# Few long-lived PSUM pools with tile-wise reuse in place of many short pools, in a linear-attention and MQA forward and backward kernel

## Chip, cores, metric

The kernel runs on one core of one Trainium2 chip. The metric is the device time of one execution in microseconds (us), slowest core, so here the only one. A profile is one more execution, read by its trace; its span can differ from the median by some us.

## The reference

Two independent blocks on 2048 tokens of width 448 in bfloat16, 16 heads of 28, their outputs side by side, and all eight gradients for a given gradient of the output:

```python
def _A_ref(x, wqkv, wo):                     # linear attention
    q, k, v = split_heads(x @ wqkv)
    pq, pk = phi(q), phi(k)                  # phi(t) = where(t > 0, t + 1, exp(t)) + 1e-6
    kv = einsum("bhsd,bhse->bhde", pk, v);  z = pk.sum(over tokens)
    o = einsum("bhqd,bhde->bhqe", pq, kv) / (einsum("bhqd,bhd->bhq", pq, z)[..., None] + 1e-6)
    return merge_heads(o) @ wo
def _B_ref(x, wq, wk, wv, wo):               # one key/value head for 16 query heads
    q = split_heads(x @ wq); k = x @ wk; v = x @ wv
    p = softmax(einsum("bhqd,bkd->bhqk", q, k) * Dh ** -0.5)
    return merge_heads(einsum("bhqk,bkd->bhqd", p, v)) @ wo
def reference(...):
    out, vjp = jax.vjp(lambda *t: concatenate([A(...), B(...)], -1), *inputs)
    return (out, *vjp(grad_out))
# ... shortened: helper names stand for the reshapes and transposes
```

## The kernel before

It is one program, phase A then phase B. TensorE (PE) multiplies and transposes into PSUM, VectorE (DVE) and ScalarE (ACT) move PSUM on to SBUF, GpSimd (POOL) clears buffers, SyncE (SP) issues most DMAs. A copy that empties a PSUM tile is called an eviction. Every small stage opens its own PSUM pool, with one set of slots for each tile name, and closes it at its end. Tiles named below: in A, ps_nd (numerator and denominator), ps_oa (out_a); in B, ps_qn (norms of the queries), otp (transposes of the attention's output), ps_ob (out_b), gwoBacc (gradient of wo), ps_do (gradient of the attention's output); in both, projT, projK, projV (projections), xTps (transposes of the last 64 columns of x or of the output's gradient), tps_set (other transposes). The stage between the forward loop and the key/value loop of B, cut:

```python
with tc.tile_pool(name="psOt", bufs=2, space=PSUM) as psOt, ...:
    for g in range(4):
        for st in range(NS):
            otp = psOt.tile([P, P], F32, name="otp")
            tpz(otp[:, :], osb_all[:, g * NS + st, :], identF)         # PE transpose
            # ... DVE: copy, denominators, reciprocal, product -> onat_B
...
    with tc.tile_pool(name="psB4", bufs=3, space=PSUM) as psB4:
        transpose_set(... oT_B ..., ... onat_B ..., psB4)
        for st in range(NS):
            ps = psB4.tile([P, D], F32, name="ps_ob")
            for g in range(4):
                mm(ps[:, :], oT_B[g][:, st * P:(st + 1) * P], woB_pr[g][:, :], start=(g == 0), stop=(g == 3))
            ot = bwk.tile([P, D], BF16, name="out_b_sb")               # two buffers
            nc.any.tensor_copy(out=ot[:], in_=ps[:, :])
            nc.sync.dma_start(out0[st * P:(st + 1) * P, D:2 * D], ot[:])
...
    with tc.tile_pool(name="psBgb", bufs=2, space=PSUM) as pst:
        transpose_64col(pst, lambda st: gb_nat[:, st, 384:448], gbT[3])        # xTps
    with tc.tile_pool(name="psBB1", bufs=1, space=PSUM) as ps7:
        accs = [ps7.tile([P, D], F32, name=f"gwoBacc{g}") for g in range(4)]
        # 64 matmuls onat_B^T gb_nat; then four copies gwo_sb and their stores
    with tc.tile_pool(name="psBB1b", bufs=2, space=PSUM) as ps1:
        # per 128 tokens: ps_do = gb wo^T on PE, six DVE operations -> don2_B
        transpose_set(... doT2_B ..., ... don2_B ..., ps1)
```

Phase A and the start and end of B are built in the same way: some thirty pools. The loops in between (forward: st_ps, oacc; key/value: s_ps, dp_ps, dvT_acc, dkT_acc; query: dpt_ps, dqacc) keep one set of pools each.

Of the kernel before, what the change touches and what calls it, by code (L numbers as in the profile page):

```python
# [12 lines left out]
BF16 = mybir.dt.bfloat16  # L13
# [8 lines left out]
SKIP_A = False  # L22


@with_exitstack
def kernel(
# [90 lines left out]
    def load_xT(pool, x2d, xn, nm):  # L117
        xT = [pool.tile([P, S], BF16, name=f"{nm}_T{c}") for c in range(4)]
        for c in range(3):
            nc.sync.dma_start_transpose(xT[c][:, :], x2d[:, c * P:(c + 1) * P])  # L120
        with tc.tile_pool(name=f"{nm}_pst", bufs=2, space=bass.MemoryType.PSUM) as pst:
            transpose_64col(pst, lambda st: xn[:, st, 384:448], xT[3])
        return xT
# [30 lines left out]
    def build_woT_pad(pool, wo_pr, nm):  # L154
        tiles = []
        with tc.tile_pool(name=f"{nm}_ps", bufs=2, space=bass.MemoryType.PSUM) as pst:
            for ci in range(4):
                lo, hi = ci * P, ci * P + DC_ROWS[ci]
                t = pool.tile([P, 512], BF16, name=f"{nm}{ci}")
                ps = pst.tile([P, 512], BF16, name="woTps")  # L160
                for g in range(4):
                    tpz(ps[0:hi - lo, g * P:(g + 1) * P], wo_pr[g][:, lo:hi], identB)
                nc.vector.tensor_copy(out=t[0:hi - lo, :], in_=ps[0:hi - lo, :])
                tiles.append(t)
        return tiles
# [47 lines left out]
    def phase_A():  # L213
        pa = ExitStack()
        ain = pa.enter_context(tc.tile_pool(name="ain", bufs=1, side="left"))
# [3 lines left out]
        woT_pad_A = build_woT_pad(ain, woA_pr, "woTA")  # L219
# [23 lines left out]
        with ExitStack() as fs:  # L243
            tmp = fs.enter_context(tc.tile_pool(name="a_tmp1", bufs=1, side="right"))
            xaT = load_xT(tmp, Ax2, xa_nat, "xa")
            wqA_pad = load_w_pad(tmp, A_wqkv, 0, "wqA_pad")
            wkA_pad = load_w_pad(tmp, A_wqkv, D, "wkA_pad", nc.gpsimd)
            wvA_pad = load_w_pad(tmp, A_wqkv, 2 * D, "wvA_pad")
            with tc.tile_pool(name="psA0", bufs=4, space=bass.MemoryType.PSUM) as ps0:
                wTq = build_wT_padrows(ain, wqA_pad, "wTqA", ps0)  # L250
                wTk = build_wT_padrows(ain, wkA_pad, "wTkA", ps0)
                wTv = build_wT_padrows(ain, wvA_pad, "wTvA", ps0)
            with tc.tile_pool(name="psA1", bufs=2, space=bass.MemoryType.PSUM) as psA1:
                def evq(g, qc, ps):
                    phi_from_psum(ps[:, :], pqT_A[g][:, qc * 512:(qc + 1) * 512], (P, 512), awk)
                proj_T(psA1, lambda dc, g, rows: wqA_pad[0:rows, dc, g * P:(g + 1) * P], xaT, evq)
                for st in range(NS):
                    ps = proj_nat(psA1, xaT, st, lambda dc, rows: wkA_pad[0:rows, dc, :], 512, nm="projK_ps")
                    phi_from_psum(ps[:, :], pkn_A[:, st, :], (P, 512), awk)
                    ps2 = proj_nat(psA1, xaT, st, lambda dc, rows: wvA_pad[0:rows, dc, :], 512, nm="projV_ps")  # L260
                    nc.scalar.activation(out=vaug_A[:, st, :], in_=ps2[:, :], func=ACT.Identity)
                nc.gpsimd.memset(vaug_A[:, :, :].rearrange("p t (h c) -> p t h c", c=32)[:, :, :, 0:1], 1.0)
# [3 lines left out]
        with tc.tile_pool(name="psA2", bufs=1, space=bass.MemoryType.PSUM) as psA2:  # L266
# [14 lines left out]
        with tc.tile_pool(name="psA3", bufs=4, space=bass.MemoryType.PSUM) as psA3:  # L281
# [14 lines left out]
        with ExitStack() as fs2:  # L296
            t2 = fs2.enter_context(tc.tile_pool(name="a_oT", bufs=1, side="right"))
            oT_A = [t2.tile([P, S], BF16, name=f"oT_A{g}") for g in range(4)]
            with tc.tile_pool(name="psA4", bufs=3, space=bass.MemoryType.PSUM) as psA4:
                transpose_set(lambda g, qc: oT_A[g][:, qc * 512:(qc + 1) * 512],  # L300
                              lambda g, st: onat_A[:, st, g * P:(g + 1) * P], psA4)
                for st in range(NS):
                    ps = psA4.tile([P, D], F32, name="ps_oa")
                    for g in range(4):
                        mm(ps[:, :], oT_A[g][:, st * P:(st + 1) * P], woA_pr[g][:, :], start=(g == 0), stop=(g == 3))
                    ot = awk.tile([P, D], BF16, name="out_a_sb")
                    nc.any.tensor_copy(out=ot[:], in_=ps[:, :])
                    nc.sync.dma_start(out0[st * P:(st + 1) * P, 0:D], ot[:])
# [3 lines left out]
        with ExitStack() as bs:  # L312
# [6 lines left out]
            with tc.tile_pool(name="psAga", bufs=2, space=bass.MemoryType.PSUM) as pst:  # L319
                transpose_64col(pst, lambda st: ga_nat[:, st, 384:448], gaT[3])  # L320
            with tc.tile_pool(name="psAB1", bufs=3, space=bass.MemoryType.PSUM) as ps1:
# [19 lines left out]
                with tc.tile_pool(name="psAB7", bufs=1, space=bass.MemoryType.PSUM) as ps7:  # L341
# [11 lines left out]
            with tc.tile_pool(name="psAB1t", bufs=4, space=bass.MemoryType.PSUM) as pst:  # L353
# [5 lines left out]
        with ExitStack() as bs:  # L359
            tp_ = bs.enter_context(tc.tile_pool(name="a_pqn", bufs=1, side="right"))  # L360
            pqn_A = tp_.tile([P, NS, 512], BF16, name="pqn_A")
            with tc.tile_pool(name="psAB2t", bufs=4, space=bass.MemoryType.PSUM) as pst:
                transpose_set(lambda g, qc: pqn_A[:, qc * 4:(qc + 1) * 4, g * P:(g + 1) * P],
                              lambda g, st: pqT_A[g][:, st * P:(st + 1) * P], pst)
            with tc.tile_pool(name="psAB2", bufs=1, space=bass.MemoryType.PSUM) as ps2:
# [13 lines left out]
            with tc.tile_pool(name="psAB2b", bufs=2, space=bass.MemoryType.PSUM) as psb:  # L379
# [12 lines left out]
        with tc.tile_pool(name="psAB3", bufs=4, space=bass.MemoryType.PSUM) as ps3:  # L392
# [11 lines left out]
        with ExitStack() as bs:  # L404
            pk1 = bs.enter_context(tc.tile_pool(name="a_gkn", bufs=1, side="right"))
            gkn_A = pk1.tile([P, NS, 512], BF16, name="gkn_A")
            with ExitStack() as bs2:
                pv = bs2.enter_context(tc.tile_pool(name="a_vaugT", bufs=1, side="right"))
                vaugT_A = [pv.tile([P, S], BF16, name=f"vaugT_A{g}") for g in range(4)]
                with tc.tile_pool(name="psAB4t", bufs=4, space=bass.MemoryType.PSUM) as pst:  # L410
                    transpose_set(lambda g, qc: vaugT_A[g][:, qc * 512:(qc + 1) * 512],
                                  lambda g, st: vaug_A[:, st, g * P:(g + 1) * P], pst)
                with tc.tile_pool(name="psAB4", bufs=2, space=bass.MemoryType.PSUM) as ps4:
# [7 lines left out]
            with tc.tile_pool(name="psAB4b", bufs=3, space=bass.MemoryType.PSUM) as ps4:  # L421
# [3 lines left out]
        with ExitStack() as bs:  # L425
            pk2 = bs.enter_context(tc.tile_pool(name="a_pkT", bufs=1, side="right"))
            pkT_A = [pk2.tile([P, S], BF16, name=f"pkT_A{g}") for g in range(4)]
            with tc.tile_pool(name="psAB4c", bufs=4, space=bass.MemoryType.PSUM) as ps4:
# [8 lines left out]
        for gT, blk in [(gqT_A, 0), (gvT_A, 2)]:  # L437
            with ExitStack() as bs:
                tp_ = bs.enter_context(tc.tile_pool(name=f"a_ab5_{blk}", bufs=1, side="right"))
                gnat = tp_.tile([P, NS, 512], BF16, name=f"gnat_{blk}")  # L440
                with tc.tile_pool(name=f"psAB5_{blk}", bufs=3, space=bass.MemoryType.PSUM) as ps5:
# [4 lines left out]
        with tc.tile_pool(name="psAB6", bufs=2, space=bass.MemoryType.PSUM) as ps6:  # L446
# [28 lines left out]
    def phase_B():  # L475
        pb = ExitStack()
        bin_ = pb.enter_context(tc.tile_pool(name="bin", bufs=1, side="left"))
# [3 lines left out]
        woT_pad_B = build_woT_pad(bin_, woB_pr, "woTB")  # L481
# [13 lines left out]
        with ExitStack() as fs:  # L495
# [3 lines left out]
            xbT = load_xT(tmp, Bx2, xb_nat, "xb")  # L499
# [9 lines left out]
            with tc.tile_pool(name="psB0", bufs=2, space=bass.MemoryType.PSUM) as ps0:  # L509
# [11 lines left out]
            with tc.tile_pool(name="psB1", bufs=2, space=bass.MemoryType.PSUM) as psB1:  # L521
# [25 lines left out]
            with tc.tile_pool(name="psB2", bufs=2, space=bass.MemoryType.PSUM) as psB2:  # L547
# [17 lines left out]
                for g in range(4):  # L565
                    for qc in range(NQC):
# [5 lines left out]
                        for j in range(4):  # L572
                            nc.scalar.activation(out=qT_B[g][32 * j:32 * j + 1, qc * 512:(qc + 1) * 512],  # L573
                                                 in_=ps[32 * j:32 * j + 1, :], func=ACT.Sqrt,
                                                 scale=kmax2_bc[32 * j:32 * j + 1, 0:1])
        if STOP_AFTER == 'B_proj':
            ron.release(); pb.close(); return
# [16 lines left out]
        with tc.tile_pool(name="qblkp", bufs=2, side="right") as qbp, \  # L594
                tc.tile_pool(name="psS", bufs=2, space=bass.MemoryType.PSUM) as psS, \
                tc.tile_pool(name="psO", bufs=2, space=bass.MemoryType.PSUM) as psO, \
# [24 lines left out]
        with tc.tile_pool(name="psOt", bufs=2, space=bass.MemoryType.PSUM) as psOt, \  # L621
                tc.tile_pool(name="owork", bufs=2, side="right") as owork:
# [14 lines left out]
        if STOP_AFTER == 'B_fwd':  # L637
            gbp.release(); ron.release(); pb.close(); return

        with ExitStack() as fs2:  # L640
            t2 = fs2.enter_context(tc.tile_pool(name="b_oT", bufs=1, side="right"))
            oT_B = [t2.tile([P, S], BF16, name=f"oT_B{g}") for g in range(4)]
            with tc.tile_pool(name="psB4", bufs=3, space=bass.MemoryType.PSUM) as psB4:
                transpose_set(lambda g, qc: oT_B[g][:, qc * 512:(qc + 1) * 512],
                              lambda g, st: onat_B[:, st, g * P:(g + 1) * P], psB4)
                for st in range(NS):
# [3 lines left out]
                    ot = bwk.tile([P, D], BF16, name="out_b_sb")  # L650
# [13 lines left out]
        with ExitStack() as bs:  # L664
            with tc.tile_pool(name="psBgb", bufs=2, space=bass.MemoryType.PSUM) as pst:
                transpose_64col(pst, lambda st: gb_nat[:, st, 384:448], gbT[3])
            with tc.tile_pool(name="psBB1", bufs=1, space=bass.MemoryType.PSUM) as ps7:
# [11 lines left out]
            with tc.tile_pool(name="psBB1b", bufs=2, space=bass.MemoryType.PSUM) as ps1:  # L679
                for st in range(NS):  # L680
                    ps = ps1.tile([P, 512], F32, name="ps_do")
                    for ci in range(4):
# [15 lines left out]
                              lambda g, st: don2_B[:, st, g * P:(g + 1) * P], ps1)  # L698
        gbp.release()
# [5 lines left out]
        with ExitStack() as ns_:  # L705
# [7 lines left out]
            with tc.tile_pool(name="psU", bufs=3, space=bass.MemoryType.PSUM) as psU, \  # L713
                    tc.tile_pool(name="psUd", bufs=2, space=bass.MemoryType.PSUM) as psUd, \
                    tc.tile_pool(name="psUacc", bufs=1, space=bass.MemoryType.PSUM) as psUacc, \
# [37 lines left out]
        with tc.tile_pool(name="qblkT", bufs=1, side="right") as qbp, \  # L753
                tc.tile_pool(name="psTd", bufs=4, space=bass.MemoryType.PSUM) as psTd, \
                tc.tile_pool(name="psTq", bufs=2, space=bass.MemoryType.PSUM) as psTq, \
# [32 lines left out]

        with ExitStack() as bs:
# [4 lines left out]
            with tc.tile_pool(name="psBB4t", bufs=3, space=bass.MemoryType.PSUM) as pst:  # L794
# [9 lines left out]
            with tc.tile_pool(name="psBB4", bufs=2, space=bass.MemoryType.PSUM) as ps4:  # L804
# [62 lines left out]
```

## Time and profile before

The time was 2883.08 us, median of 6 runs (2879.93 to 2890.67). The profiled execution had a span of 2881.5 us at a mean granted TensorE clock of 0.948 (the share of the full clock that the chip let TensorE have). Added up from the stage table that the prediction shows in part:

| part of the span | us | what is full |
|---|---|---|
| start to first projT (loads) | 49.1 | DMA |
| phase A from there to the last ps_gx | 357.3 | PE or DVE in turn |
| B up to the first oacc | 147.0 | PE, then ACT (64 square roots) |
| forward loop | 563.1 | ACT |
| last oacc to first s_ps ("mid stage") | 135.4 | DVE in two of its four parts |
| key/value and query loops | 1577.5 | PE, then DVE |
| end | 52.1 | PE |

### The profile page before, as it was taken

The numbers are of one execution on the slowest core, as the hardware profiler recorded it, in microseconds if no ns is written. First come the engines' busy times: TensorE is split into PE (matmuls) and PEld (weight loads), VectorE is DVE, ScalarE is ACT, GpSimd is POOL, SyncE is SP. The second block draws the span as 40 slices with busy tenths as digits, with TensorE's granted clock in tenths as the row PEclk, the third lists the DMA queues.
The fourth block names the chain that finished last, engine by engine and source line by source line (L and its number), as shares of the span: only waits on it lengthen the run. The fifth ranks groups of instructions, "written<-read, shape, count | busy, mean of one in ns | idle before, by whom it ended". The sixth has DMA issues, their size and how long they took to land. (4 is left out here: it accounts for less than half of the span.)

```text
span 2881.5 us, 35266 instructions
## 1 busy us (share of the span) xinstructions
PE 2516.0 (87%) x11290; PEld 1065.9 (37%) x11290; DVE 1709.0 (59%) x3495; ACT 1516.4 (53%) x2434; POOL 210.1 (7%) x310
## 2 busy tenths in 40 slices
PE   4766879798888887789999999999998887878788
PEld 1233533233333333334444444444443333333334
DVE  3757502122222225487777777777776998989893
ACT  1210113998888884136666666666665444444343
POOL 1000002022222221000000000000000000000000
PEclk9987988699999997889999999999999999999999
DMA  6020220366666663100000000000000776767672
GB/s 70 1 73 6 40 63 1 110 241 240 241 241 239 240 240 125 32 1 1 1 1 1 1 1 1 1 1 1 1 1 23 218 239 208 239 208 240 206 239 85
DMA packets 266987, 296.65 MB, mean 103 GB/s; under 512 B 66464, under 2 KB 217536, under 8 KB 266800
## 3 DMA queue, kind: packets, MB, share of 16 engines
q1 hardware_dynamic: 246016, 226.82, 25.8%
q0 software_dynamic: 20784, 67.58, 6.4%
q8 instruction: 88, 1.44, 0.2%
q14 instruction: 99, 0.81, 0.1%
HBM read 144.02 MB, written 144.02 MB: 100 GB/s over the span
## 5 line engine op out<-in xcount | busy, mean ns | idle before, releaser
L731 DVE TENSOR_TENSOR ds_sb<-dp_ps,e 128x512 bf16<-128x512 f32 x1024 | 686.3, 692 | 251.1 <-PE s_ps L85 158.3
L727 ACT ACTIVATE e<-s_ps 128x512 bf16<-128x512 f32 x1024 | 583.5, 596 | 403.6 <-DVE ds_sb L731 281.7
L609 ACT ACTIVATE e<-st_ps 128x1024 bf16<-128x1024 f32 x512 | 499.0, 1022 | 64.7 <-PE st_ps L85 57.6
L85 PE MATMUL dpt_ps<-dblkT,vT_rep 128*128 128x512 bf16 x1024 | 388.6, 383 | 100.0 <-ACT dpt_sb L777 56.6
L780 DVE TENSOR_TENSOR dsT<-dpt_ps,eT 128x512 bf16<-128x512 f32 x704 | 450.3, 687 | 2.9 <-PE dpt_ps L85 2.9
L85 PE MATMUL dp_ps<-vblk,doT_B 128*128 128x512 bf16 x1024 | 387.2, 378 | 0.0
L85 PE MATMUL dkT_acc<-ds_sb,qn_B 128*128 128x512 bf16 x1024 | 385.6, 377 | 0.5 <-DVE ds_sb L731 0.3
L85 PE MATMUL dvT_acc<-e,don_B 128*128 128x512 bf16 x1024 | 385.0, 379 | 0.3 <-ACT e L727 0.3
L85 PE MATMUL dqacc<-dsT,kn_rep 128*128 128x512 bf16 x1024 | 379.4, 381 | 2.1 <-DVE dsT L780 1.5
L85 PE MATMUL oacc<-e,vaug_rep 128*128 128x512 bf16 x1024 | 304.1, 378 | 65.1 <-ACT e L609 62.0
L85 PE MATMUL s_ps<-kblk,qT_B 128*128 128x512 bf16 x1024 | 346.5, 379 | 0.8 <-DVE doT_B L102 0.8
L777 ACT ACTIVATE dpt_sb<-dpt_ps 128x512 bf16<-128x512 f32 x320 | 191.0, 597 | 292.8 <-PE dpt_ps L85 290.8
L85 PE MATMUL st_ps<-qblk,kT_rep 128*128 128x512 bf16 x1024 | 305.3, 380 | 3.5 <-ACT qT_B L573 3.5
L601 DVE MEMSET qblk<- 128x512 uint32 x32 | 15.5, 485 | 459.0 <-PE st_ps L85 408.2
L85 PEld LDWEIGHTS <-vaug_rep 128*128 128x128 bf16 x1024 | 98.6, 96 | 245.9 <-issue 185.4
L85 PEld LDWEIGHTS <-kn_rep 128*128 128x128 bf16 x1024 | 99.8, 97 | 240.1 <-issue 157.0
L615 POOL DMA_DIRECT2D edram<-e x256 | 138.4, 541 | 487.5 <-ACT e L609 487.3
L85 PEld LDWEIGHTS <-vT_rep 128*128 128x128 bf16 x1024 | 99.7, 98 | 163.6 <-DVE dblkT L211 27.0
L85 PEld LDWEIGHTS <-qT_B 128*128 128x128 bf16 x1024 | 99.1, 97 | 159.7 <-issue 66.1
L778 DVE TENSOR_TENSOR dsT<-dpt_sb,eT 128x512 bf16<-128x512 bf16 x320 | 134.8, 421 | 30.2 <-ACT dpt_sb L777 29.6
L85 PEld LDWEIGHTS <-don_B 128*128 128x128 bf16 x1024 | 98.4, 96 | 135.8 <-issue 43.3
L85 PEld LDWEIGHTS <-kT_rep 128*128 128x128 bf16 x1024 | 98.6, 96 | 128.1 <-issue 6.8
(271 smaller groups left out, 1915.0 us busy)
## 6 DMA issues: line engine op xcount, KB each, us to landing
eT<-edram SPq DMA_DIRECT2D x512, 256.0 KB
edram<-e POOLq DMA_DIRECT2D x256, 256.0 KB, 2.3
edram<-e SPq DMA_DIRECT2D x256, 256.0 KB
xa_nat<-in_A_x_dram SPq DMA_DIRECT2D x1, 1792.0 KB
out_dram<-out_a_sb SPq DMA_DIRECT2D x16, 112.0 KB
ga_nat<-in_grad_out_dram SPq DMA_DIRECT2D x1, 1792.0 KB
out_dram<-gx_sb SPq DMA_DIRECT2D x16, 112.0 KB
xb_nat<-in_B_x_dram SPq DMA_DIRECT2D x1, 1792.0 KB
```

Of the source, the lines that this page charges most:

```text
L85: nc.tensor.matmul(out_ap, lhsT=lhsT, rhs=rhs, start=start, stop=stop, tile_position=(0, 0))
L601: nc.vector.memset(qblk[:], 0.0)
L609: nc.scalar.activation(out=e[:], in_=st_ps[:, :], func=ACT.Exp, scale=scale)
L615: eng.dma_start(edram[r0:r0 + P, :], e[:, :])
L727: nc.scalar.activation(out=e[:], in_=s_ps[:, :], func=ACT.Exp, scale=scale)
L731: nc.vector.tensor_tensor(out=ds_sb[:, :], in0=dp_ps[:, :], in1=e[:, :], op=ALU.mult)
L777: nc.scalar.activation(out=dpt_sb[:, :], in_=dpt_ps[:, :], func=ACT.Identity)
L778: nc.vector.tensor_tensor(out=dsT[:, :], in0=dpt_sb[:, :], in1=e, op=ALU.mult)
L780: nc.vector.tensor_tensor(out=dsT[:, :], in0=dpt_ps[:, :], in1=e, op=ALU.mult)
```

## The change

Its intent: a stage should not have to wait until the whole pool of the stage before is released. Few pools live through a phase; tiles of many names share one tag's slots; a slot taken again waits only for the tile that held it; and the two output buffers get six slots. No matmul, copy or byte is added or taken away. The core (the same edit is made at every pool; cut):

```diff
+class SharedPs:
+    def __init__(self, pool, tag): ...
+    def tile(self, shape, dtype, name=None, **kw):
+        return self.pool.tile(shape, dtype, name=(name or "pst"), tag=self.tag, **kw)
 def phase_A():
+    psApool = pa.enter_context(tc.tile_pool(name="psA", bufs=4, space=PSUM, reuse_waits="tile"))
+    gen = SharedPs(psApool, "gen")
+    acc4 = SharedPs(psApool, "acc4")
...
-            with tc.tile_pool(name="psA1", bufs=2, space=PSUM) as psA1:
+                psA1 = gen
-        with tc.tile_pool(name="psA2", bufs=1, space=PSUM) as psA2:
+            psA2 = acc4
...
-                    ot = awk.tile([P, D], BF16, name="out_a_sb")
+                    ot = awk.tile([P, D], BF16, name="out_a_sb", bufs=6)
...
 def phase_B():
+    psB_pre = tc.alloc_tile_pool(name="psBpre", bufs=8, space=PSUM, reuse_waits="tile")
+    genB = SharedPs(psB_pre, "gen")
...
-        with tc.tile_pool(name="psOt", bufs=2, space=PSUM) as psOt, \
-                tc.tile_pool(name="owork", bufs=2, side="right") as owork:
+        psB_mid = tc.alloc_tile_pool(name="psBmid", bufs=4, space=PSUM, reuse_waits="tile")
+        genM = SharedPs(psB_mid, "gen")
+        accM = SharedPs(psB_mid, "acc4")
+        psOt = genM
...
-                    ot = bwk.tile([P, D], BF16, name="out_b_sb")
+                    ot = bwk.tile([P, D], BF16, name="out_b_sb", bufs=6)
-            with tc.tile_pool(name="psBB1", bufs=1, space=PSUM) as ps7:
+                ps7 = accM
...
+        psB_post = pb.enter_context(tc.tile_pool(name="psBpost", bufs=8, space=PSUM, reuse_waits="tile"))
# ... and reuse_waits="tile" on the pools of the three loops
```

## The prediction

> **What bounds the kernel now**
>
> I read first the page's busy shares and slices, then one table of busy time by stage (boundaries taken from where the TensorE timeline changes tile name), then the timeline of TensorE and VectorE at the boundaries, and last the static instruction order of both built programs.
>
> ```profile
> PE 2516.0 (87%) x11290; PEld 1065.9 (37%) x11290; DVE 1709.0 (59%) x3495; ACT 1516.4 (53%) x2434; POOL 210.1 (7%) x310
> ...
> PE   4766879798888887789999999999998887878788
> ...
> PEclk9987988699999997889999999999999999999999
> ```
>
> No engine bounds the whole span; it is a row of stages. The 40 slices are 72 us each: the first seven and slices 15 to 17 are where TensorE has holes. The stage table says which engine is full in each (columns: length, busy us and count of PE, weight loads, DVE, ACT, POOL, then granted clock, DMA share, GB/s):
>
> ```profile
> core 0: us, PE busy (x) PEld busy (x) DVE busy (x) ACT busy (x) POOL busy (x), PEclk, DMA share, GB/s
> 49.00:116.60 67.60, 56.02 (x192) 16.34 (x191) 58.74 (x96) 28.18 (x49) 1.22 (x1) 0.97 0.00 1
> 135.40:157.40 22.00, 7.88 (x64) 5.85 (x65) 21.54 (x59) 0.00 (x0) 0.00 (x0) 0.54 0.00 1
> 157.40:180.40 23.00, 18.30 (x128) 11.04 (x127) 7.60 (x23) 7.35 (x14) 0.00 (x0) 0.92 0.19 62
> 180.40:188.80 8.40, 0.00 (x0) 0.00 (x0) 0.00 (x0) 1.06 (x2) 0.00 (x0) 0.77 0.99 281
> 406.40:430.00 23.60, 8.53 (x57) 5.34 (x57) 5.41 (x13) 2.13 (x4) 1.70 (x4) 0.58 0.35 100
> 550.00:1116.50 566.50, 501.41 (x2048) 197.25 (x2048) 111.80 (x399) 500.28 (x513) 138.03 (x256) 0.99 0.66 242
> 1116.50:1153.60 37.10, 21.81 (x65) 11.36 (x64) 36.64 (x260) 0.00 (x0) 0.37 (x1) 0.55 0.03 10
> 1153.60:1181.30 27.70, 19.08 (x128) 11.36 (x128) 7.20 (x25) 8.03 (x16) 0.00 (x0) 0.92 0.19 63
> 1181.30:1203.50 22.20, 16.31 (x80) 8.36 (x80) 2.20 (x5) 1.60 (x3) 0.00 (x0) 0.82 0.06 17
> 1203.50:1252.00 48.50, 32.94 (x129) 12.32 (x129) 45.06 (x102) 0.00 (x0) 6.93 (x1) 0.68 0.01 3
> 1252.00:2226.00 974.00, 972.80 (x4352) 420.12 (x4351) 712.55 (x1074) 587.74 (x1040) 0.14 (x1) 1.00 0.01 2
> 2226.00:2829.60 603.60, 501.75 (x2048) 199.50 (x2048) 545.98 (x1040) 258.57 (x573) 27.56 (x4) 0.97 0.73 222
> ```
>
> Three loops hold 566.5 + 974.0 + 603.6 = 2144 us, 74%: the forward exponentials (ACT about full), the key/value gradients (PE full), the query gradients (DVE nearly full). Everything else, 737 us, is phase A and the small stages of B. There an engine is full in some stages and idle in the next: the stages hand over one after another.
>
> How they hand over (start, length, engine, instruction, idle before and what ended it):
>
> ```profile
> 157.48 1.44 PE L89 MATMUL tps_set<-identB,onat_A 128*128 128x128 bf16 x12 [5.21 <-DVE nsb L287]
> 188.88 1.03 PE L89 MATMUL xTps<-identB,ga_nat 128*64 128x128 bf16 x8 [8.53 <-DMA ga_nat<-in_grad_out_dram]
> 430.00 20.62 PE L85 MATMUL projT_ps<-xb_T,wqB_pad 128*128 128x512 bf16 x64 [0.48 <-DVE wvTB L518]
> 1181.31 0.72 PE L89 MATMUL xTps<-identB,gb_nat 128*64 128x128 bf16 x8 [4.58 <-ACT out_b_sb L651]
> 1203.52 5.71 PE L85 MATMUL ps_do<-woTB,gbT 128*128 128x512 bf16 x12 [5.17 <-ACT gwo_sb L675]
> ```
>
> The reader is to see that in the first, fourth and fifth the releaser is an eviction of the previous stage's PSUM, not the input that the instruction reads: xTps reads gb_nat, whose load was issued at 546.5, and waits for out_b_sb. That is a pool boundary. The second line is a real data wait.
>
> **What the Trainium skill says**
>
> "PSUM — Partial Sum Buffer", section "PSUM bank collisions raise a hardware error": a bank that one engine reads must not be written by another at the same time, so reuse must be guarded bank by bank. Guarding by bank is what the change leaves; waiting for a whole pool is more than needed. The five lines agree that more is waited for.
>
> "TensorE: Matmul & The Clock Gate", section "What's actually happening": an idle PE falls to half clock after an idle window of about 3.4 us and needs about as long of work to return. The table agrees: 0.54 and 0.55 in the two stages where PE is half empty, 1.00 in the full loop. So holes over 3 us cost something afterwards too, and a stage limited by DVE does not care.
>
> "DMA: Bandwidth & Descriptors", section "Anatomy of one DMA": a fixed part of about 2 us per DMA, mostly completion. With two output buffers two tiles then take a bit over 2 us: the trace has two ps_oa tiles every 2.31 us (167.86, 170.18, 172.50), of which PE works 1.67.
>
> **The change part by part**
>
> It changes no matmul, copy or byte. It (a) lets stages share PSUM slots, with waits tile by tile, (b) gives most small stages 4 or 8 slots, though one tag now serves names that had slots each, (c) gives out_a_sb and out_b_sb 6 buffers instead of 2. SBUF pools keep their boundaries. The built order of the three big loops is the same, waits included, but for their first instructions. So 0 from 2144 us.
>
> Phase A. *Projection, 49 to 116.7*: now the order is 16 projT, then projK and projV in turn. projT becomes DVE-bound: 16 x 1.80 us (the cadence of the projK rows here) from 51.1 gives 79.9; then PE-bound, 8 matmuls of 0.2685 = 2.15 us per block, the last projV ends near 111.4. The ones column of vaug (POOL, 1.22 us) now follows late, so kvzacc starts near 113.4 instead of 116.67: gain 3. *Numerator to out_a*: DVE must do 22.0 us plus 16 oT copies of 0.37 = 28; copies now mix in, and ps_oa, 64 x 0.187 = 12 us plus some 2.4 at cold clock, ends 41 us after the start of ps_nd, before 44.9: gain 4. The 8.4 us load of ga_nat stays: its SBUF still waits for oT_A. *Go stage to dkvz, 188.8 to 264.7*: one gwo_sb copy leaves DVE (1.72 idle + 0.62), gndT copies fill holes of 0.57, dkvzacc starts under the transposes (7 of 64 matmuls, and no 0.94 wait): gain 5. *dq, dk*: DVE-bound and gapless but for 0.1 + 0.5 + 0.7: gain 1.5. *Weight gradients, 301 to 370*: the 0.66 waits go, but transposes no longer interleave with matmuls: 0. Phase A: 13.5.
>
> B up to the forward loop. projT waited behind woTps, which waits for woB_pr's DMAs to 420.64. Now xTps and wTps go between them: xTps near 416.5, first projT near 422.6, six done and the last woTps by 425.7; before, 430.0 plus 2.6 for six: gain 7. The key-norm chain runs before the qn matmuls: 4 norms, reduce (2.27), broadcast, table load end near 500.6 instead of 505.46: gain 4.8. First scores no longer wait for the last square root (549.95 to 551.04): 1. Sum 13.
>
> B between forward loop and key/value loop, 1116.5 to 1252. gwoBacc (14.6 us, with 0.5 before and the 5.17 behind) now runs two matmuls per two otp under a stage that DVE fills (36.6 of 37.1): 20.3 gone, 1 given back. out_b with 6 buffers: PE 12 us instead of about 16 from 1160.7: 4. The 4.58 wait goes. From ps_do on, DVE has 45 of 48.5: 1 to 2. By stage: 2.4 + 35.7 + 6 + 12 + 3 + 47 = 106 against 135.5: gain 29; I take 28 for the four gwo_sb copies that now stand ahead of out_b on ACT.
>
> Tail: ps_dvn needn't wait for dqT (1.19) or mix with the transposes: 1.4.
>
> Sum 13.5 + 13 + 28 + 1.4 = 56. I take off 1 to 2 us for hand-overs that I priced without semaphore latency: 2883 - 55 = 2828 us, or 1.9%.
>
> **The rivals**
>
> 1. *Less slot supply, not more.* projT, projK and projV had two slots each, six banks, now four in common; tps_set and ps_oa had three each. If the shared ring makes PE wait for a slow reader, phase A gives back its 13.5: 2840. For: the order has lost its interleaving there. Against: the readers (0.37 and 0.6 us) keep up with four slots.
> 2. *The wait moves on.* The ga_nat load, woB_pr's DMAs and the SBUF pools are untouched; what arrives earlier may only wait longer there. Half the gain of phase A and B's start lost: about 2842.
> 3. *Clock.* Fuller PE keeps its clock up. Six small stages have 0.5 to 0.7; if those not DVE-bound run at 1.0, 5 to 8 us more: 2821.
> 4. *The gwoBacc overlap costs.* At half clock two otp and two gwoBacc take about 1.35 us against DVE's 1.08; 30 pairs x 0.27 = 8 if PE never warms: 2836.
>
> **Range and chances**
>
> The mid stage of B carries half and is the surest, because its waits name evictions. Phase A is a sum of small terms, each uncertain by half. I put 8 in 10 on 2814 to 2846. The 2% line lies at about 2826, two us from my number, so faster is a little under even: 0.43; same 0.55; slower 0.02, since no loop of weight changes.
>
> **What would show it**
>
> Right: the three loops keep 566, 974 and 604 us within 1; from the last oacc to the first s_ps about 107; the first projT of B about 15 us after the last ps_gx (before 24); kvzacc 64 us after the first projT (before 67.6); no out_b_sb or gwo_sb as releaser of xTps or ps_do. Wrong: a loop longer by more than 2 us (its rhythm then depended on the pools), 8 us or more of new PE waits on projT_ps or tps_set slots, or an otp stage much over 38 us.

## More of the kernel before

The runs were made on several chips of this kind, on which the median of the kernel before lay between 2875.5 and 2885.5 us; a ratio is always to the kernel before in the same rounds on the same chip, so ratios compare runs better than medians do.

## The result

The changed kernel took 2819.63 us, median of 8 runs (2811.34 to 2831.42), beside 2884.32 us for the kernel before (16 runs). The ratio is 0.9773, 95% interval 0.9755 to 0.979: faster by 2.3%. Here and below a ratio is the mean time of one kernel's fast runs over that of the other's of the same rounds, so not quite the ratio of the medians. A saving "by time" below is one minus the ratio, times the median of before.

The page of the changed kernel: busy shares, then TensorE and its granted clock in 40 slices.

```profile
PE 2482.3 (88%) x11290; PEld 1058.1 (38%) x11290; DVE 1706.0 (61%) x3497; ACT 1514.1 (54%) x2432; POOL 210.3 (7%) x310
...
PE   3877989588888888799999999999998878878789
...
PEclk9978999799999999799999999999999999999999
```

The instruction count of PE is the same, and PE's busy time fell by 34 us although no matmul is gone: matmuls at half clock take longer, and there are fewer of those (of the 32 ps_qn, 32 ran at half clock before, at 1.06 to 1.22 us each, and 8 in the changed profile; at full clock one takes 0.59); the span's mean clock rose from 0.948 to 0.963. The stage table of the changed kernel, columns as in the prediction's:

```profile
56.10:119.20 63.10, 53.57 (x192) 15.73 (x192) 57.95 (x96) 28.32 (x50) 1.22 (x1) 1.00 0.00 1
138.00:179.80 41.80, 29.73 (x192) 19.20 (x191) 28.85 (x80) 7.98 (x15) 0.00 (x0) 0.68 0.11 36
397.40:413.35 15.95, 6.21 (x53) 4.25 (x53) 3.42 (x8) 1.90 (x4) 1.70 (x4) 0.68 0.51 147
524.00:1088.50 564.50, 499.77 (x2047) 197.27 (x2047) 111.80 (x399) 500.67 (x516) 138.13 (x256) 0.99 0.64 238
1088.50:1190.30 101.80, 77.76 (x402) 38.19 (x401) 88.65 (x387) 10.64 (x20) 7.25 (x2) 0.86 0.08 26
1190.30:2165.00 974.70, 972.15 (x4338) 419.06 (x4339) 713.39 (x1074) 587.42 (x1039) 0.00 (x0) 1.00 0.00 1
2165.00:2771.30 606.30, 504.51 (x2064) 201.31 (x2062) 547.07 (x1042) 258.79 (x573) 27.70 (x4) 0.97 0.73 222
```

The fifth row is the mid stage: nearly the same DVE work (88.65 us; 91.10 before) now takes 101.8 us instead of 135.4. The TensorE timeline of the changed kernel at the hand-overs that the prediction showed, and at the first s_ps (start, length, instruction, idle before and what ended it):

```profile
156.74 1.68 PE L100 MATMUL tps_set<-identB,onat_A 128*128 128x128 bf16 x12 [1.72 <-DVE nsb L307]
188.40 1.88 PE L100 MATMUL xTps<-identB,ga_nat 128*64 128x128 bf16 x16 [8.55 <-DMA ga_nat<-in_grad_out_dram]
407.28 0.72 PE L100 MATMUL woTps<-identB,woB_pr 128*128 128x128 bf16 x4 [9.74 <-DMA woB_pr<-in_B_wo_dram]
413.35 1.68 PE L96 MATMUL projT_ps<-xb_T,wqB_pad 128*128 128x512 bf16 x6
1092.02 0.57 PE L96 MATMUL gwoBacc<-gb_nat,onat_B 128*128 128x448 bf16 x2 [0.28 <-DVE onat_B L677]
1142.81 1.12 PE L100 MATMUL xTps<-identB,gb_nat 128*64 128x128 bf16 x16
1143.85 6.51 PE L96 MATMUL ps_do<-woTB,gbT 128*128 128x512 bf16 x24
1190.26 1.46 PE L96 MATMUL s_ps<-kblk,qT_B 128*128 128x512 bf16 x3 [8.02 <-DVE kblk L224]
```

gwoBacc starts 3.5 us into the otp part instead of 67 us after its start; xTps and ps_do of B start without a wait; the two load waits (ga_nat, woB_pr) stand as they did, and a new wait of 8.02 us has come up before the key/value loop. It is not an added cost: kblk was built on DVE before too, between the doT copies, and is now built after them, on an engine whose one gap there (0.80 us, before kblk is cleared) was there before too.

Stage by stage, from the start times of the named tiles in each trace (us):

| stage | before | changed | gain | predicted |
|---|---|---|---|---|
| start to first projT (loads) | 49.1 | 56.1 | -7.0 | 0 |
| projection (to first kvzacc) | 67.6 | 63.2 | 4.4 | 3 |
| first ps_nd to last ps_oa | 44.8 | 41.7 | 3.1 | 4 |
| xTps of ga to first ps_dq | 75.8 | 70.6 | 5.2 | 5 |
| ps_dq, ps_dk | 36.8 | 33.2 | 3.6 | 1.5 |
| weight gradients, rest of A | 132.4 | 132.7 | -0.3 | 0 |
| B: last ps_gx to first oacc | 147.0 | 131.0 | 16.0 | 13 |
| forward loop | 563.1 | 560.1 | 3.0 | 0 |
| mid stage | 135.4 | 101.8 | 33.6 | 28 |
| key/value and query loops | 1577.5 | 1581.0 | -3.5 | 0 |
| end | 52.1 | 48.5 | 3.6 | 1.4 |

The column of gains sums to 61.7; the spans differ by 61.8 (rounding). Three rows are chance, as the runs below show: over 14 profiles of kernels with the same loads the first projT came between 45.6 and 56.1 us, the forward loop took 559.9 to 564.5 us, and in the 12 with unchanged loops the key/value and query loops took 1577.5 to 1581.8 us.

### The profile page after: what moved, and what is told of

Its sections match the earlier page's. It is cut to its first block, busy times and chain, and to the rows that moved or that the text cites. A ratio compares the mean times of both kernels' runs of the same rounds, so it can differ in the third digit from the quotient of the medians.

```text
span 2819.7 us, 35250 instructions
## 1 busy us (share of the span) xinstructions
PE 2482.3 (88%) x11290; PEld 1058.1 (38%) x11290; DVE 1706.0 (61%) x3497; ACT 1514.1 (54%) x2432; POOL 210.3 (7%) x310
## 4 chain that ended last, share of the span: by engine, by line
PE 71%; ACT 14%; DVE 6%; issue 4%; SPq 1%; DMA 1%; POOL 1%; ACTq 0%; POOLq 0%; DVEq 0%
PE dkT_acc L96 10%; ACT e L650 9%; PE dp_ps L96 9%; PE dpt_ps L96 9%; PE s_ps L96 8%; PE dvT_acc L96 8%; PE dqacc L96 7%; PE oacc L96 5%; PE st_ps L96 4%; ACT dqT_B L832 2%; ACT qT_B L613 2%; PE gw_acc L96 1%; PE tps_set L100 1%; ACT dpt_sb L826 1%; PE ps_gx L96 1%
## 5 line engine op out<-in xcount | busy, mean ns | idle before, releaser
L650 ACT ACTIVATE e<-st_ps 128x1024 bf16<-128x1024 f32 x512 | 497.5, 1023 | 63.2 <-PE st_ps L96 63.0
L656 POOL DMA_DIRECT2D edram<-e x256 | 138.4, 541 | 478.9 <-ACT e L650 478.7
```

Source lines behind the costliest of these rows:

```text
L650: nc.scalar.activation(out=e[:], in_=st_ps[:, :], func=ACT.Exp, scale=scale)
L656: eng.dma_start(edram[r0:r0 + P, :], e[:, :])
```

## The experiments

The change is three things at once: shared slots, waits by tile, more output buffers. Comparing the built programs' instruction lists first showed something that the diff does not: tile-wise waits alone leave the instruction order of every engine as it was, and taking them out of the changed kernel leaves its order as it is. Only sharing the slots moves instructions. That matters because, as the Trainium skill's page "PSUM — Partial Sum Buffer", section "Engine vs sequencer instructions", has it, ScalarE, VectorE and GpSimd queues are strict first in, first out, and matmuls start in program order: an instruction that stands behind a waiting one can't pass. The traces agree: in the first run below the waits were by tile and gwoBacc's inputs were complete when the otp part ended near 1146 us, yet it started at 1168.8, in its old place behind out_b and xTps.

So theory O: the new order is the gain, and sharing is what makes it. Rival W: the waits by tile are the gain. Rival B: the output buffers are. One more is not tested: sharing also gives most stages more slots (four or eight instead of two or three), and no run gives the short pools more slots.

### Waits by tile alone

```diff
-with tc.tile_pool(name="psOt", bufs=2, space=PSUM) as psOt
+with tc.tile_pool(name="psOt", bufs=2, space=PSUM, reuse_waits="tile") as psOt
# ... and so on every PSUM pool of the kernel before
```

> The short pools of the kernel before are kept, each with its own slots; only their waits are changed, so that a reused bank waits for the tile that held it and not for the whole pool before. The built program then has the instruction order of the kernel before on every engine, only waits differ. Theory O (the gain comes from the new order of instructions, which sharing slots allows): 5 to 14 us faster, from the 4.58 us wait of xTps and part of the 5.17 us wait of ps_do and a few of about 0.5 us; gwoBacc still runs behind out_b. Rival W (the gain comes from the waits being bank by bank): 45 to 62 us faster.

Measured: 2865.51 us, ratio 0.9941 (0.9928 to 0.9953): 17 us faster by time, more than theory O's 14 and far from W's 45. The mid stage took 123.5 us. Its TensorE timeline, three lines:

```profile
1161.48 1.67 PE L85 MATMUL ps_ob<-woB_pr,oT_B 128*128 128x448 bf16 x8 [0.68 <-ACT out_b_sb L651]
...
1167.01 0.63 PE L89 MATMUL xTps<-identB,gb_nat 128*64 128x128 bf16 x8
...
1184.68 2.20 PE L85 MATMUL ps_do<-woTB,gbT 128*128 128x512 bf16 x7
```

Both boundary waits (4.58 and 5.17 us) are gone, but ps_ob still stops 0.68 us after every two tiles, and gwoBacc stops once, 1.76 us, for the last out_b_sb. Outside the mid stage the old order gained too: the projection took 63.6 us, within 0.4 of the changed kernel's 63.2, and the way from B's last ps_gx to the first oacc 138.4, beside 147.0 before.

### Six output buffers alone

```diff
-ot = awk.tile([P, D], BF16, name="out_a_sb")
+ot = awk.tile([P, D], BF16, name="out_a_sb", bufs=6)
# ... and so for out_b_sb
```

> The kernel before with six buffers instead of two for out_a_sb and out_b_sb and nothing else. By my step for out_b (PE 12 us instead of about 16) and the same in out_a with the 8.4 us load behind it: 4 to 8 us faster. Rival B (most of what the two output stages gain comes from the buffers, not from the pools): 12 us or more.

Measured: 2870.09 us, ratio 0.9957 (0.9943 to 0.9971): 12.4 us faster by time. My 4 to 8 was too low; rival B's 12 is met, though as a share of the whole it is not "most". The mid stage took 123.6 us, as with the waits by tile, for other reasons:

```profile
1154.18 11.01 PE L85 MATMUL ps_ob<-woB_pr,oT_B 128*128 128x448 bf16 x56
1165.85 0.61 PE L89 MATMUL xTps<-identB,gb_nat 128*64 128x128 bf16 x8 [0.66 <-ACT out_b_sb L651]
...
1185.46 0.58 PE L85 MATMUL ps_do<-woTB,gbT 128*128 128x512 bf16 x1 [5.17 <-ACT gwo_sb L675]
```

Now ps_ob runs through, and the wait of xTps shrinks from 4.58 to 0.66 with the pool boundary still there; the 5.17 us wait before ps_do stays. So the 4.58 us had two causes in series: xTps waited for the whole pool, and the last eviction in that pool waited for a buffer whose store was still under way. Either remedy removes it. The 5.17 us had only the boundary, the 0.68 us stops only the buffers. In phase A, first ps_nd to last ps_oa took 40.4 us, shorter than in the changed kernel.

### Both, without sharing

The two edits above together; the instruction order is still that of short pools.

> The kernel before with bank-by-bank waits on its short pools and six buffers for out_a_sb and out_b_sb, but no shared slots: the instruction order stays that of short pools. If the two remedies were independent, 17 us and 12 us would add to 29 us. Theory O2 (both take away the same 4.6 us wait of xTps and the same store-bound hold of out_b, so they overlap): 20 to 25 us faster than before, last oacc to first s_ps 117 to 121 us; the remaining 40 us to the changed kernel are then the order of instructions alone.

Measured: 2847.06 us, ratio 0.9886 (0.9866 to 0.9905): 32.8 us faster, so the whole is not under the sum of 17.0 and 12.4 and theory O2's 20 to 25 falls. The mid stage did overlap (115.7 us: 19.8 us gained where 11.9 and 11.8 add to 23.7), slightly under the 117 to 121 expected. The interval (27 to 39 us by time) and the first projT at 45.6 us in the profile leave the rest to chance or to small overlaps elsewhere that I did not separate. About half of the change's 65 us can be had without touching the order. What sharing adds, new order and more slots together, is the other half, some 33 us by time: theory O holds for that half alone.

### Sharing without waits by tile

```diff
-tc.tile_pool(name="psA", bufs=4, space=PSUM, reuse_waits="tile")
+tc.tile_pool(name="psA", bufs=4, space=PSUM)
# ... and so on every pool of the changed kernel
```

> The changed kernel with every pool put back to waiting for the whole pool before it; slots stay shared inside a few long-lived pools. The built program has the instruction order of the changed kernel on every engine. Theory O: 58 to 66 us faster than before, so within 4 us of the changed kernel, since only three pool boundaries are left in all of B and none in A. Rival W: under 20 us faster.

Measured: 2824.19 us, ratio 0.9788 (0.9772 to 0.9805): 61 us faster, as theory O expected. Waits by tile add about 4 us once slots are shared, which is not clear of the noise (give or take 7 by the two intervals): inside one pool a slot waits for its own tile anyway. (The "three pool boundaries" of the expectation was a miscount; B has five.) This run holds the new order, the freer slots and the six buffers together, so it does not show the order alone. Rival W falls as the main cause, with a correction: on short pools the waits by tile are worth 17 us. The two are two roads to part of the same gain.

### The mid stage alone

```diff
# the kernel before, with
-with tc.tile_pool(name="psOt", bufs=2, space=PSUM) as psOt, ...
+psB_mid = tc.alloc_tile_pool(name="psBmid", bufs=4, space=PSUM, reuse_waits="tile")
+genM = SharedPs(psB_mid, "gen"); accM = SharedPs(psB_mid, "acc4"); psOt = genM
# psB4, psBgb, psBB1b -> genM; psBB1 -> accM; output buffers stay at two
```

> The kernel before with the change in one stage alone: shared slots with bank-by-bank waits from the end of the forward loop to the start of the key/value loop, output buffers left at two. If the stages add up: the stage between the last oacc and the first s_ps is 101 to 108 us instead of 135, the time 26 to 33 us less; without the six output buffers some 2 to 4 us of it are missing, as out_b waits for its stores. If the shared PSUM pools in the other parts are what starts this stage sooner, under 20 us.

Measured: 2854.99 us, ratio 0.9903 (0.989 to 0.9916): 28 us faster; mid stage 105.95 us. It stands by itself, and the missing 4.1 us to 101.8 are the buffers (3.7 us in the run with two buffers below).

### Phase A alone, and the two ends of B alone

```diff
# phase A of the changed kernel, phase B of the kernel before
+psApool = pa.enter_context(tc.tile_pool(name="psA", bufs=4, space=PSUM, reuse_waits="tile"))
```

> The change in phase A alone (shared slots, bank-by-bank waits, six buffers for out_a_sb), phase B as before. If the parts add up: 14 to 18 us faster than before, first projT to first ps_gx 305 us instead of 321, and phase B keeps its lengths of before (135 us from the last oacc to the first s_ps). Rival (the parts of phase A only move the wait on to the loads at the start of phase B): under 8 us, with a longer wait for woB_pr at the start of B.

Measured: 2865.21 us, ratio 0.9934 (0.9917 to 0.995): 19 us faster by time, a little over the expected 14 to 18; first projT to first ps_gx 304.4 us. B kept its lengths: 23.4 us from the last ps_gx to the first projT, 135.0 us mid stage. The rival falls: the load waits at the start of B did not grow.

And the other way round, the two outer pools of B alone:

```diff
# the kernel before, with
+psB_pre = tc.alloc_tile_pool(name="psBpre", bufs=8, space=PSUM, reuse_waits="tile")
+psB_post = pb.enter_context(tc.tile_pool(name="psBpost", bufs=8, space=PSUM, reuse_waits="tile"))
```

> The change in phase B before the forward loop and after the query loop alone; phase A, the stage between the forward and key/value loops and the loops as before. Adding up what the profiles of the changed kernels have there against those of the unchanged ones: 13 us from the end of ps_gx to the first oacc (131 to 135 us instead of 145 to 147) and 3.5 us after the last dqacc (48.5 instead of 52): 14 to 19 us faster. Rival (the gain at the start of B needs phase A to end sooner): under 8 us.

Measured: 2865.96 us, ratio 0.9962 (0.9941 to 0.9982): 11 us by time (5 to 17), 135.9 us from the last ps_gx to the first oacc, 50.0 us after the last dqacc. The interval reaches both the expected 14 to 19 and the rival's 8, so the time does not decide; the stage does: B's start gained 10 us on the 145.9 of the profiles with this part unchanged, with phase A as long as before. The parts add: 19.0 + 28.0 + 10.9 and some 4 for out_b's buffers make 62, beside 65.5 by time for the change.

### The changed kernel with two output buffers

```diff
-ot = bwk.tile([P, D], BF16, name="out_b_sb", bufs=6)
+ot = bwk.tile([P, D], BF16, name="out_b_sb")
# ... and so for out_a_sb
```

> The changed kernel with two buffers instead of six for out_a_sb and out_b_sb. By the prediction's steps only out_b loses (4 us) and the numerator stage keeps its 4 us, which were put down to the copies mixing in: about 4 us slower than the changed kernel, first ps_nd to last ps_oa 41 to 42 us. Theory S (each output stage is held by its stores, in A too; the run with six buffers alone had already 40.4 us there against 44.8): 8 to 9 us slower, first ps_nd to last ps_oa 45 to 47 us, last oacc to first s_ps 105 to 107 us.

Measured: 2834.83 us (2823.08 to 2838.73), ratio 0.9819 (0.9796 to 0.9842). Against the changed kernel's 0.9773 that is some 13 us, give or take 8 by the two intervals; its profiled run, the fastest of the four, lost 5.7 us in the two stages: first ps_nd to last ps_oa 43.7 us (2.0 more), mid stage 105.5 (3.7 more). Between the two expectations: the buffers do count in A, but by 2 us of the 3.1 gained, not by all (up to 2.9 beside three other profiles with six buffers and the new order, which took 40.8 to 41.0). The longer medians are not explained by the stages of one profile; that stays open.

### gwoBacc behind out_b again

```diff
-psB_mid = tc.alloc_tile_pool(name="psBmid", bufs=4, space=PSUM, reuse_waits="tile")
-accM = SharedPs(psB_mid, "acc4")
+psB_mid = tc.alloc_tile_pool(name="psBmid", bufs=8, space=PSUM, reuse_waits="tile")
+accM = genM
```

> The changed kernel with the four gwoBacc accumulators in the same ring of slots as the other tiles of that stage (eight slots instead of two times four). The built program then has gwoBacc behind out_b again, as before the change, while everything else of the stage stays. By my step for the overlap (20.3 us gone, 1 given back, of which 5 were a wait that stays gone): last oacc to first s_ps 114 to 122 us instead of 101.8, the time 12 to 20 us over the changed kernel. Rival (VectorE bounds the whole stage, so the place of gwoBacc matters little): under 6 us over.

Measured: 2831.2 us, ratio 0.9813 (0.9798 to 0.9828); mid stage 111.96 us, so 10.2 us for the place of gwoBacc, between my 12 to 20 and the rival's 6. (The other tiles have eight slots here instead of four; out_b took the same 12.3 us.) The timeline of that run:

```profile
1138.90 12.28 PE L96 MATMUL gwoBacc<-gb_nat,onat_B 128*128 128x448 bf16 x64
1151.01 4.35 PE L96 MATMUL ps_do<-woTB,gbT 128*128 128x512 bf16 x15
```

On a warm PE gwoBacc costs 12.3 us, not 14.6 and a wait of 5; and without it the otp part took 33.3 us instead of 35.2, so hiding it costs 1.9 us there. The difference, 10.4 us, is the net within 0.2.

### Two slots instead of four in phase A

```diff
-gen = SharedPs(psApool, "gen")
+gen = SharedPs(psApool, "gen", 2)      # tile(..., bufs=2) for this tag
```

> The changed kernel with two slots instead of four in the general ring of phase A; all else as changed. Rival 1 of the prediction (slot supply) with numbers: if the readers keep up, as I argued, first projT to first ps_gx stays within 6 us of the changed kernel's 305 us. If the slots of the shared ring are what lets TensorE run ahead of its readers, phase A loses more than its whole gain of 15 us, 320 us or more, and the run is 15 to 35 us slower than the changed kernel.

Measured: 2847.71 us, ratio 0.9904 (0.9888 to 0.9921): over the changed kernel by 28 us in medians, by some 38 in ratios; first projT to first ps_gx 333 us, 12 more than the kernel before. The projection took 72.3 us instead of 63.2, the weight gradients 81.2 instead of 68.9. Of what ended TensorE's waits in phase A (sum, times, longest):

```profile
PE ps_nd L97 <- DVE nsb L308: 11.3, 8, 1.9
PE projT_ps L97 <- DVE phi_r L215: 9.0, 13, 0.9
```

The changed kernel has 8.8 and 5.6 us there; these two lines are 6 of the 28 us that phase A lost, and I did not add up the shorter waits. So rival 1 named a real mechanism, and four slots are what keeps it away: one shared tag with two slots is worse than separate names with two each.

### Past both kernels

The changed kernel's trace names three waits that are left: ga_nat (8.55 us), kblk (8.02 us), and four waits of dpt_ps for dblkT, 34.3 us in all, since the block matrix of each head group is cleared and filled only when the group before is done with its one buffer. The edits, cut:

```diff
-dblk = qbp.tile([P, NS, 512], BF16, name="dblkT")            # one buffer, whole group
+dblk = qbp.tile([P, 4, 512], BF16, name="dblkT")             # quarters, six slots; the next
+# group's quarters are cleared and filled on GpSimd during this group
+# kblk, vblk in quarters too: cleared on GpSimd, the first filled on ScalarE
+# ga_nat, gaT allocated and loaded before ps_nd (nsb and gn take over the slots of phi_m, phi_r)
```

> The changed kernel and three more edits against the waits that its trace shows: ga loaded under the numerator stage (8.5 us of waiting for ga_nat), kblk and vblk built in four pieces off VectorE (8.0 us before the first s_ps), dblkT in pieces with the next group's pieces built during the present one (34.3 us of TensorE waits before dpt_ps). If each of these waits ends the stage it stands in: 35 to 50 us faster than the changed kernel, 2770 to 2785 us. If VectorE, nearly full in the query loop, sets its pace, or GpSimd is too slow at copies: 10 to 25 us faster.

Measured: 2763.71 us, ratio 0.9584 (0.9566 to 0.9602), 56 us under the changed kernel in medians (55 in ratios): more than expected. xTps of ga starts 0.1 us after the last ps_oa; the mid stage took 93.1 us; the query loop 571.7 instead of 594.6. One wait was left, before the first dpt_ps: 9.6 us, or 12.0 from the last dkT_acc. DVE and GpSimd there (GpSimd clearing quarters, DVE filling the first; the fourth line is from a little later, when GpSimd was idle):

```profile
2131.24 11.10 POOL L818 MEMSET dblkT<- 128x2048 bf16 x6 [955.10 <-PE dp_ps L96]
2133.07 7.52 DVE L224 COPY dblkT<-doT_B 32x512 bf16<-32x512 bf16 x4 [2.61 <-POOL dblkT L818]
2141.90 2.55 DVE L224 COPY dblkT<-doT_B 32x512 bf16<-32x512 bf16 x4
```

```profile
2148.92 1.17 DVE L224 COPY dblkT<-doT_B 32x512 bf16<-32x512 bf16 x4
```

Four copies took 7.52 us beside the memsets, one copy for one memset in turn; 2.55 us after them, where GpSimd's own copies (0.60 us each) took turns with them; and 1.17 us alone. The Trainium skill's page "SBUF — State Buffer", section "SBUF: two separate sides", says that a DVE instruction in a mode that uses two ports and a GpSimd instruction share a port pair under an exclusive lock held for a whole instruction; 1.85 to 1.88 us for a copy that takes 0.27 to 0.29 us alone, beside memsets of 1.8 to 1.9 us, agrees. (The trace does not name the mode of a copy.)

The last version builds the first two quarters inside the key/value loop, all quarters on GpSimd alone, and loads xb_nat and woB_pr during the weight gradients:

```diff
+                    if t in (8, 9):                      # key/value loop
+                        dblks.append(make_dblk(t - 8, qbpA))
...
         rq.release()                                     # phase A, after ps_dq
+        bx = tc.alloc_tile_pool(name="bx", bufs=1, side="right")
+        pre_B += [bx, load_x(bx, Bx2, "xb"), load_wo_padrows(bx, B_wo, "woB_pr")]
```

> The run best3 and two more edits: the first two pieces of dblkT are built inside the key/value loop (12.0 us of gap before the first dpt_ps in best3), and xb_nat and woB_pr are loaded during the weight gradients of phase A (16 us from the last ps_gx to the first projT of B). If both waits end there: 2745 to 2756 us. If the next loads (xb_T, wqB) only take over the second wait: 2752 to 2760 us. If GpSimd's copies hold the key/value loop: no faster than best3.

Measured: 2749.83 us, ratio 0.9554 (0.9532 to 0.9575), 4.5% under the kernel before. From the last dkT_acc to the first dpt_ps it took 2.3 us instead of 12.0, and the query loop took 564.1 us. The start of B gained nothing (18.6 us from the last ps_gx to the first projT): TensorE now waited 10.3 us for wqB_pad, so the remaining loads of B took over that wait, as the second expectation had it. The time lies in the first expectation's range all the same: this chip's kernel before was 7 us faster than the first pair's, and by its ratio the time would be 2756 there, so the time alone does not choose between the two.

## Why the prediction was right

The time fell in the range (2819.6 in 2814 to 2846), 8 us below the number, and past the 2% line at 2826, to which the prediction gave 0.43; the class that it held likelier (same, 0.55) did not come. The mechanism held, and so did the largest term. The sizes were too low in most terms, and taking off 1 to 2 us at the end made it worse. By its steps:

- *Loops, 0.* Right. The formal sign against it, "a loop longer by more than 2 us", did come up (key/value loop 2.7 us longer by first s_ps and last dkT_acc), but the kernel with six buffers alone, whose loops are untouched, shows 3.1 us. One profile's loop length is uncertain by 2 to 3 us, and the sign was set too fine.
- *Phase A, 13.5.* 16.0 in the pair of traces. The projection gained 4.4 instead of 3, but the working put it down to the new order of projT, projK and projV, and the old order with waits by tile took 63.6 us there: that the order is the cause is not shown. ps_dq and ps_dk gained 3.6 instead of 1.5. The numerator's 4 came out near (3.1), but its cause was put wrong: the prediction credited copies that mix in; taking the six buffers back costs 2.0 to 2.9 us, and six buffers alone gave 4.4 with the old order. The prediction read two ps_oa tiles in 2.31 us as a store limit, and then counted it for out_b only. (The section that it cites for 2 us describes DMAs issued from GpSimd; SyncE issues these. The trace has 2.1 us from the end of the first copy, 165.2, to the copy that its store's landing released, 167.3.)
- *B up to the forward loop, 13.* 16.0 in the pair of traces, but by chance: four profiles with this part unchanged (145.9 us in the mean) and five with it changed (133.4 us) give 12.5. About half of that comes with waits by tile and the old order too (138.4 and 140.2 us in the two profiles). The kernel before had all 32 ps_qn matmuls at half clock in its profile; of the five other profiles with its order one had 32, four had 28.
- *Mid stage, 28.* 33.6, the largest miss. The sum 2.4 + 35.7 + 6 + 12 + 3 + 47 counts the way from the last oacc to the first otp twice: 2.4 and 35.7 came to 35.2 together (2.9 of the miss). The 3 us around xTps were 1.1, the 47 after it 46.4, the 6 were 6.9, and the 1 us taken off for gwo_sb copies did not show. "PE 12 us" for out_b was exact (12.1). The 20.3 for gwoBacc was right for what goes between xTps and ps_do, but in two parts: a boundary wait of 5.2, which goes without any new order, and 15 us of work and a small wait, of which the new place of gwoBacc saves 10.2 net on a warm PE.
- *End, 1.4.* 3.6. The 1.19 us wait of ps_dvn was in the sum, though ps_dvn still waits 0.80 us for dqT_B; what was not is that eight slots let the 64 dqT transposes run in 3.75 us without a stop. Three slots needed 5.5 us for the last 58, of which 0.7 are chance: in that profile a half-clock stretch of 3.41 us fell on them, and without one (the run of the mid stage alone) they needed 4.8. With eight slots such a stretch makes 5.37 us of the 3.75, in four of eight profiles.
- *"That is a pool boundary."* Half right for the 4.58 us: six buffers without touching a pool take all but 0.66 of it away as well.

The rivals: the first (slots) is true at two slots and does not bite at four. The second (the wait moves on to loads) falls: ga_nat's wait was 8.5 us before and after, woB_pr's 9.5 and 9.7. The third (clock) is part of the gain, as PE's busy time shows, but I did not measure its share. The fourth (overlap costs 8 us) cost 1.9: PE was warm, clock 0.95 in the otp part.

The tight point was the chance. The 2% line was 2 us from the number, and nearly all terms were lower bounds from waits named in the trace; neither the clock nor the freer slots had a term of their own.

## What to carry to other kernels

A pool boundary costs twice: the wait at the boundary, and the order, since work written behind it can't be placed under an earlier stage that leaves an engine idle. Look for stages where one engine is full and another half empty, give their tiles disjoint slots in one long-lived pool with enough slots (here four, not two), and let independent matmuls move in. When the named releaser of a wait is an eviction, ask what that eviction waited for: here a store, so that more output buffers removed the same wait.

## What the Trainium skill lacked or had wrong

- "SBUF — State Buffer": nothing wrong; its lock between DVE and GpSimd showed here with a number: 32x512 copies of 1.88 us under GpSimd memsets, 0.28 us alone.
- "TensorE: Matmul & The Clock Gate", section "What's actually happening": its window of about 3.4 us agrees (in the kernel before's trace every stretch between two changes of the clock is a whole multiple of 3.413 us), and so does its remark that the phase varies by run; what it costs a stage was seen here: 28 or all 32 of the 32 ps_qn matmuls at half clock in profiles of one and the same order.
- No page has how busy TensorE must be to keep its full clock. In the otp part of the kernel before it stood at half clock for 37.5 us on end with no idle stretch over 0.7 us in it (busy 59% of the part); with gwoBacc between the otp it was busy 82% and the clock 0.95.
- None of the pages that I read has the spread of the load phase: with the same DMAs the first projT came at 45.6 to 56.1 us in 14 profiles, later by and large the longer the queue of SP stood before the woA_pr loads behind the two DMA transposes (2.3 us in the earliest, 4.5 us in the kernel before's profile, 9.6 us in the latest, the changed one's).
